# Storing the MoE output through 32x32 VectorE transposes, with a new order of the output matmuls

## The chip, the cores and the metric

The kernel runs on one core of one Trainium2 chip. The metric is the device time of one execution in microseconds; lower is better. Ratios are the mean time of one kernel's runs over that of the kernel before in the same rounds, so a ratio is not quite the ratio of the medians quoted beside it.

Engines: PE is TensorE (matmuls), PEld its weight loads, ACT is ScalarE, DVE is VectorE, POOL is GpSimd, SP issues DMAs.

## The reference, cut to what matters

```python
def reference(q, kv, w_sr, moe_w_in, moe_w_out):
    x = attention(q, pooled(kv) @ w_sr)      # 4 x 12288 queries of 128 channels, 768 keys each
    x = x.reshape(49152, 128)
    h = x @ moe_w_in                         # 128 -> 2048
    g = h * (1.0 / (1.0 + np.exp(-1.702 * h)))
    return (g @ moe_w_out).astype(np.float32)   # 2048 -> 128
```

The kernel computes everything transposed: channels lie on the 128 partitions, tokens along the free dimension. So the last matmul leaves the output of 512 tokens as `[128 channels, 512 tokens]` in one PSUM bank, while the result in memory has one row of 128 channels per token. Something has to transpose it.

## The kernel before: the parts that matter

The work is cut into units of three 128x512 matmuls. A unit is filled (three matmuls into a PSUM tile of three banks), passed through ACT (exp in the attention, gelu in the MoE) and drained (three more matmuls that accumulate in a bank of `ring`). There are 192 attention units and then 512 MoE units; a token group of 512 tokens is 16 chunks, so 5.33 MoE units. The PSUM tile `big` has two buffers: PE may fill unit n+2 only when ACT is done with unit n.

```python
    def fill_moe(t):
        h_ps = big.tile([128, K, 512], F32, name="big")            # K = 3, two buffers
        for k in range(K):
            g, fc = divmod(K * t + k, FCH)                         # FCH = 16
            nc.tensor.matmul(h_ps[:, k, :], w_in_sb[:, fc * 128:(fc + 1) * 128],
                             xs[g // 4][:, (g % 4) * G:(g % 4 + 1) * G], start=True, stop=True)
        a = agpool.tile([128, K, 512], BF, name="ag")
        nc.scalar.activation(a, h_ps, AF.Gelu_apprx_sigmoid)
        g_of[t] = a

    def drain_moe(t):
        todo = list(late)
        late.clear()
        a = g_of.pop(t)
        for k in range(K):
            # ... o_of[g] = ring.tile(...) at the first chunk of a group
            nc.tensor.matmul(o_of[g], w_out_sb[:, fc, :], a[:, k, :],
                             start=(fc == 0), stop=(fc == FCH - 1))
            if fc == FCH - 1:
                oT = opool.tile([128, 128, 4], BF, name="oT")
                nc.vector.tensor_copy(oT.rearrange("p a b -> p (a b)"), o_of[g])
                late.append((g, oT))
        for g, oT in todo:
            store(g, oT)

    def store(g, oT):
        o_ps = o_of.pop(g)[:, 0:256].bitcast(BF)
        for gi in range(4):
            nc.tensor.transpose(o_ps[:, gi * 128:(gi + 1) * 128], oT[:, :, gi], ident)
        o_sb = opool.tile([128, 4, 128], F32, name="o_sb", bufs=3)
        nc.vector.tensor_copy(o_sb.rearrange("p a b -> p (a b)"), o_ps)
        nc.sync.dma_start(out=out_r[g], in_=o_sb)
```

In the order of steps, drains run ten units (L) behind in the attention. From the first MoE step on, two attention drains are issued per step until none is left; MoE drains start five units behind, and every sixteenth step has a second one until the distance is zero.

```python
    for n in range(NA + NM):
        fill(n + 2)
        for _ in range(2 if n >= NA else 1):
            if done_a < NA and n - L >= done_a - (L if n >= NA else 0):
                drain_attn(done_a // 2, done_a % 2)
                done_a += 1
        # ... sums of exps every eighth step, side work of the attention
        if n >= NA + L // 2:
            for _ in range(2 if n % 16 == 0 else 1):
                if done_m <= n - NA:
                    drain_moe(done_m)
                    done_m += 1
```

I call a drain beyond one per step an **extra drain**: ten are needed in either kernel to come from a distance of ten to none.

The softmax here doesn't subtract the row's maximum and nothing guards it: scores larger than these inputs give would overflow.

Of the kernel before, what the change touches and what calls it, by code (L numbers as in the profile page):

```python
# [7 lines left out]
F32 = mybir.dt.float32  # L8
BF = mybir.dt.bfloat16
# [10 lines left out]
def kernel(  # L20
    ctx, tc, q, kv, w_sr, moe_w_in, moe_w_out, out,
):
    nc = tc.nc
    B, N, C = q.shape
    _, H, W, _ = kv.shape
# [16 lines left out]
    q_bf = nc.dram_tensor("q_bf", (B * N, C), BF, kind="Internal").ap()  # L42

    kv_r = kv.rearrange("b (ch p) (a w) c -> b a ch p (w c)", p=128, a=2)
    out_r = out.rearrange("(g p i) c -> g p i c", p=128, i=4)

    L = 10

# [4 lines left out]
    qpool = ctx.enter_context(tc.tile_pool(name="qpool", bufs=3))  # L53
    agpool = ctx.enter_context(tc.tile_pool(name="ag", bufs=14))
    npool = ctx.enter_context(tc.tile_pool(name="norm", bufs=5))
    opool = ctx.enter_context(tc.tile_pool(name="op", bufs=2))
    big = ctx.enter_context(tc.tile_pool(name="big", bufs=2, space=bass.MemoryType.PSUM))
    ring = ctx.enter_context(tc.tile_pool(name="ring", bufs=2, space=bass.MemoryType.PSUM))

# [14 lines left out]
    def pool_kv(b, a):  # L74

        ps = ring.tile([128, 512], F32, name="ring")
        ts = [kv_tiles.pop((b, a, ch)) for ch in range(HC)]
        order = ([(ch, w) for ch in range(HC) for w in range(r)] if b == 0 else
                 [(ch, w) for w in range(r) for ch in range(HC)])
        for ch, w in order:  # L80
            if (b, a, w) == (0, 0, 0) and ch > 0:
                warm(4)
            nc.tensor.matmul(ps[32 * ch:32 * ch + 32, :], mean4, ts[ch][:, w],  # L83
                             start=(w == 0), stop=(w == r - 1))
        pooled[b, a] = kvtmp.tile([Hp, 4, C], BF, name="pooled")
        nc.vector.tensor_copy(pooled[b, a].rearrange("p a c -> p (a c)"), ps[:Hp, :])  # L86

    def transpose_pooled(b, a):
        ps = ring.tile([128, 4, Hp], BF, name="ring")
        t = pooled.pop((b, a))  # L90
        for wp in range(4):
            nc.tensor.transpose(ps[:, wp, :], t[:, wp, :], ident[:Hp, :Hp])  # L92
        pTs[b, a] = kvtmp.tile([128, h], BF, name="pT")
        nc.vector.tensor_copy(pTs[b, a], ps.rearrange("p a b -> p (a b)"))

    def make_k(b, a):
        ps = ring.tile([128, 512], F32, name="ring")
        if a == 0:
            kTs[b] = kvres.tile([128, J], BF, name="kT")
        nc.tensor.matmul(ps[:, :h], w_sr_sb, pTs[b, a], start=True, stop=True)  # L100
        nc.vector.tensor_copy(kTs[b][:, a * h:(a + 1) * h], ps[:, :h])

    def make_v(b, a):
        ps = ring.tile([128, 512], F32, name="ring")
        if a == 0:
            vs[b] = kvres.tile([128, JC, C], BF, name="v")
        pT = pTs.pop((b, a))
        for k in range(K):
            nc.tensor.matmul(ps[:, k * C:(k + 1) * C], pT[:, k * 128:(k + 1) * 128], w_sr_sb,
                             start=True, stop=True)  # L110
        nc.vector.tensor_copy(vs[b][:, a * K:(a + 1) * K, :].rearrange("p k c -> p (k c)"), ps[:, :h])
# [18 lines left out]
    def transpose_q(g):  # L130
        s = g // 4
        if g % 4 == 0:
            qTs[s] = qpool.tile([128, 1, SG], BF, name="qT")
        ps = ring.tile([128, 4, 128], BF, name="ring")
        for i in range(4):
            o = (g % 4) * G + i * 128
            nc.tensor.transpose(ps[:, i, :], xs[NS // 2 + s][:, o:o + 128], ident)  # L137
        dst = qTs[s][:, 0, (g % 4) * G:(g % 4 + 1) * G].rearrange("p (t i) -> p t i", i=4)
        src = ps.rearrange("p i t -> p t i")
        if g < 3:  # L140
            nc.scalar.copy(dst, src)  # L141
        else:
            nc.vector.tensor_copy(dst, src)  # L143
# [22 lines left out]
    ident = cpool.tile([128, 128], BF)  # L166
    nc.vector.memset(ident, 0.0)
    for m in range(0, 128, 32):
        p = slice(m, m + 32)
# [34 lines left out]
    def fill_attn(i, t):  # L204
        b, s = i // GB, i // 4
        s_ps = big.tile([128, K, 512], F32, name="big")
        rhs = qTs[s][:, 0, (i % 4) * G:(i % 4 + 1) * G]
        for k in range(K):
            jc = K * t + k
            nc.tensor.matmul(s_ps[:, k, :], kTs[b][:, jc * 128:(jc + 1) * 128], rhs,  # L210
                             start=True, stop=True)
        a = agpool.tile([128, K, 512], BF, name="ag")
        nc.scalar.activation(a, s_ps, AF.Exp, scale=scale)  # L213
        a_of[i, t] = a

    def drain_attn(i, t):
        b, s = i // GB, i // 4
        if t == 0:
            av_of[i] = ring.tile([128, 512], F32, name="ring")
        for k in range(K):  # L220
            jc = K * t + k
            nc.tensor.matmul(av_of[i], vs[b][:, jc, :], a_of[i, t][:, k, :],  # L222
                             start=(jc == 0), stop=(jc == JC - 1))
        del a_of[i, t]
        if t == 1:
            nc.vector.tensor_tensor(xs[s][:, (i % 4) * G:(i % 4 + 1) * G],  # L226
                                    av_of.pop(i), rb_of.pop(i), MUL)
# [23 lines left out]
    def background(i):  # L251

        b, gb, s = i // GB, i % GB, i // 4
        if i % 4 == 0:
            if 3 <= s + 2 < NS:
                load_qT(s + 2)
            if 4 <= s + 3 < NS:
                cast_q(s + 3)
        if b + 1 < B and gb in loads:
            a, ch = divmod(loads.index(gb), HC)  # L260
            load_kv(b + 1, a, ch)
        if i == 40:
            nc.gpsimd.dma_start(out=w_in_sb, in_=moe_w_in)
        if i == 64:
            nc.gpsimd.dma_start(out=w_out_sb, in_=moe_w_out.rearrange("(o p) c -> p o c", p=128))
# [12 lines left out]


    g_of, o_of = {}, {}  # L280
    late = []

    def fill_moe(t):
        h_ps = big.tile([128, K, 512], F32, name="big")
# [6 lines left out]
        g_of[t] = a  # L291

    def drain_moe(t):
        todo = list(late)
        late.clear()
        a = g_of.pop(t)
        for k in range(K):
            g, fc = divmod(K * t + k, FCH)
            if fc == 0:
                o_of[g] = ring.tile([128, 512], F32, name="ring")  # L300
            nc.tensor.matmul(o_of[g], w_out_sb[:, fc, :], a[:, k, :],  # L301
                             start=(fc == 0), stop=(fc == FCH - 1))
            if fc == FCH - 1:
                oT = opool.tile([128, 128, 4], BF, name="oT")
                nc.vector.tensor_copy(oT.rearrange("p a b -> p (a b)"), o_of[g])  # L305
                late.append((g, oT))
        for g, oT in todo:
            store(g, oT)

    def store(g, oT):  # L310
        o_ps = o_of.pop(g)[:, 0:256].bitcast(BF)
        for gi in range(4):
            nc.tensor.transpose(o_ps[:, gi * 128:(gi + 1) * 128], oT[:, :, gi], ident)  # L313
        o_sb = opool.tile([128, 4, 128], F32, name="o_sb", bufs=3)
        nc.vector.tensor_copy(o_sb.rearrange("p a b -> p (a b)"), o_ps)  # L315
        nc.sync.dma_start(out=out_r[g], in_=o_sb)

    NA = 2 * NG
    NM = NG * FCH // K
# [4 lines left out]
    def fill(n):  # L324
        if n < NA:
            i, t = units[n]
            if n % 2 == 0:
                background(n // 2)
            if n < 8:
                if n == 1:  # L330
                    transpose_q(3)
                if n == 2:
                    make_v(0, 0)
                if n == 4:
                    pool_kv(0, 1)
                    transpose_pooled(0, 1)
                    make_k(0, 1)
                if n == 6:
                    make_v(0, 1)
                if n == 7:  # L340
                    transpose_q(4)
                    transpose_q(5)
            fill_attn(i, t)
        elif n < NA + NM:
            fill_moe(n - NA)


    fill(0)
    fill(1)
    done_a = done_m = 0  # L350
    for n in range(NA + NM):
        fill(n + 2)
        for _ in range(2 if n >= NA else 1):
            if done_a < NA and n - L >= done_a - (L if n >= NA else 0):
                drain_attn(done_a // 2, done_a % 2)
                done_a += 1
        if n < NA and n % 8 == 7:
            sums(n // 8)
        elif n < NA and n % 2 == 1:
            if n in (9, 11):  # L360
                transpose_q(6 + (n - 9) // 2)
            extra(n // 2)
        if n >= NA + L // 2:
            for _ in range(2 if n % 16 == 0 else 1):
                if done_m <= n - NA:
                    drain_moe(done_m)
                    done_m += 1
    assert done_a == NA and done_m == NM
    for g, oT in late:
        store(g, oT)  # L370


# [28 lines left out]
```

## Time and profile before

| | before |
|---|---|
| time, median | 1023.45 us at first (3 runs); 1023.14 us with one run more |
| span of the profiled execution | 1021.7 us |
| busy: PE / ACT / DVE | 999.7 / 959.1 / 262.3 us |
| MoE: end of the first gelu to end of the last | 322.41 to 1015.88 us, 511 gaps |
| end of the last gelu to the end | 5.79 us |

PE and ACT are both nearly full, and busy shares can't rank two engines that pipeline their instructions: a recorded matmul lasts 0.38 us while matmuls start every 0.216. The paces have to be found from single instructions. Two more lines matter later. The first is the gelu's line of the view by source line, with smallest, median and largest duration in ns; the second is a stretch of the ACT timeline (start, length, number of instructions in the uninterrupted run).

```profile
L290 ACT ACTIVATE ag<-big x512: 1445/1556/1606, 321.0 to 1014.3; 128x1536 bf16<-128x1536 f32 x171
```

The run of 24, cut off by the window of the view, begins with a gelu recorded with 1.445 us, the second after a long gap (the first after a wait or a long gap is recorded with 1.450 us and the next with 1.445).

### The profile page before, as it was taken

To read this page: it belongs to the slowest core of one execution; us is meant where nothing else is said; L and a number is where in the kernel's file an instruction comes from. 1 tells how busy PE (TensorE), PEld (TensorE's weight loads), DVE (VectorE), ACT (ScalarE), POOL (GpSimd) and SP (SyncE) were. 2 spreads that over 40 slices of the span, in tenths; PEclk is the share of its full clock that TensorE was granted. 3 is DMA by queue.
4 is the path that set the end of the run, shared out by engine and by line. 5 is a ranking of instruction groups with operands and counts; after the bars stand their busy time and mean duration, and the time that the engine had idled before them with its cause. 6 is when DMAs were issued, how large, how long until landed. Compare 5 with 4: busy or idle time off the path is not lost.

```text
span 1021.7 us, 13264 instructions
## 1 busy us (share of the span) xinstructions
PE 999.7 (98%) x5298; PEld 457.9 (45%) x5398; DVE 262.3 (26%) x417; ACT 959.1 (94%) x709; POOL 92.6 (9%) x151
## 2 busy tenths in 40 slices
PE   7899999999999999999999999999999999999998
PEld 2344444444444444444444444444444444444443
DVE  3344344344334111221212111111212111111212
ACT  3888988988998999999999999999999999999997
POOL 3132332332222000000000000000000000000000
PEclk8999999999999999999999999999999999999999
DMA  9984784896500001101010110101010110101011
GB/s 189 185 145 83 145 165 83 145 158 90 83 21 1 31 32 42 42 31 42 31 42 32 41 42 32 42 31 42 32 42 31 42 42 31 42 31 42 31 42 42
DMA packets 67230, 63.84 MB, mean 62 GB/s; under 512 B 50176, under 2 KB 51328, under 8 KB 66816
## 3 DMA queue, kind: packets, MB, share of 16 engines
q0 software_dynamic: 7440, 26.22, 14.2%
q1 hardware_dynamic: 59728, 36.77, 13.3%
q8 instruction: 42, 0.69, 0.3%
q14 instruction: 20, 0.16, 0.1%
HBM read 52.49 MB, written 36.70 MB: 87 GB/s over the span
## 4 chain that ended last, share of the span: by engine, by line
PE 93%; ACT 3%; DVE 1%; issue 1%; DMA 1%; POOL 0%; ACTq 0%; DVEq 0%; POOLq 0%
PE big L287 31%; PE ring L301 30%; PE ring L222 12%; PE big L210 12%; PE ring L234 3%; ACT ag L290 3%; PE ring L313 2%; DMA x<-in_kv_dram 1%; PE ring L83 1%; ACT ag L213 1%; DVE x L226 0%; ACTq L396 0%; DVE oT L305 0%; DVE pooled L86 0%; PE ring L92 0%
## 5 line engine op out<-in xcount | busy, mean ns | idle before, releaser
L290 ACT ACTIVATE ag<-big 128x1536 bf16<-128x1536 f32 x512 | 690.0, 1546 | 4.9 <-PE big L287 4.5
L287 PE MATMUL big<-x,w_in_sb 128*128 128x512 bf16 x1507 | 412.5, 379 | 2.3
L301 PE MATMUL ring<-ag,w_out_sb 128*128 128x512 bf16 x1496 | 406.9, 379 | 1.9 <-ACT ag L290 0.5
L213 ACT ACTIVATE ag<-big 128x1536 bf16<-128x1536 f32 x192 | 264.8, 1464 | 37.3 <-PE big L210 36.6
L301 PEld LDWEIGHTS <-w_out_sb 128*128 128x128 bf16 x1536 | 150.0, 98 | 181.8 <-issue 0.7
L287 PEld LDWEIGHTS <-w_in_sb 128*128 128x128 bf16 x1536 | 145.8, 98 | 163.5 <-issue 8.0
L305 DVE CAST oT<-ring 128x512 bf16<-128x512 f32 x96 | 66.4, 692 | 451.0 <-PE ring L301 451.0
L210 PE MATMUL big<-qT,kT 128*128 128x512 bf16 x548 | 155.0, 384 | 5.6 <-DVE qT L143 2.0
L222 PE MATMUL ring<-ag,v 128*128 128x512 bf16 x573 | 154.6, 379 | 1.7 <-DVE x L226 1.1
L226 DVE TENSOR_TENSOR x<-ring,rb 128x512 bf16<-128x512 f32 x96 | 66.4, 692 | 159.0 <-PE ring L222 157.7
L315 DVE CAST o_sb<-ring 128x512 f32<-128x512 bf16 x96 | 66.4, 692 | 101.7 <-PE ring L313 101.7
L222 PEld LDWEIGHTS <-v 128*128 128x128 bf16 x576 | 56.2, 98 | 71.2 <-issue 5.3
L210 PEld LDWEIGHTS <-kT 128*128 128x128 bf16 x576 | 53.3, 98 | 76.3 <-issue 17.7
L246 POOL PARTITION_BROADCAST rb<-t x96 | 66.6, 797 | 220.2 <-DVE t L243 220.2
L313 PEld LDWEIGHTS <-oT 128*128 128x128 bf16 x384 | 32.2, 113 | 22.7 <-DVE oT L305 1.9
L313 PE MATMUL ring<-ident,oT 128*128 128x128 bf16 x384 | 37.2, 219 | 0.9 <-DVE oT L305 0.8
L234 PE MATMUL ring<-ag,ones 128*32 128x512 bf16 x576 | 35.5, 381 | 0.0
L234 PEld LDWEIGHTS <-ones 128*32 128x32 bf16 x576 | 13.2, 96 | 20.6 <-issue 10.2
L239 DVE STREAM_TRANSPOSE t<-ring 128x512 f32<-128x512 f32 x24 | 17.2, 717 | 18.8 <-PE ring L234 18.8
L243 DVE STREAM_TRANSPOSE t<-t 128x512 f32<-128x512 f32 x24 | 17.1, 712 | 2.5
L141 ACT COPY qT<-ring 128x512 bf16<-128x512 bf16 x3 | 1.8, 585 | 13.8 <-PE ring L137 13.8
L117 POOL DMA_DIRECT2D q_bf<-in_q_dram x22 | 11.4, 519 | 4.1 <-DMA x<-in_kv_dram 2.8
(41 smaller groups left out, 95.9 us busy)
## 6 DMA issues: line engine op xcount, KB each, us to landing
out_dram<-o_sb SPq DMA_DIRECT2D x96, 256.0 KB, 2.0
q_bf<-in_q_dram POOLq DMA_DIRECT2D x22, 512.0 KB, 7.3
kvt<-in_kv_dram POOLq DMA_DIRECT2D x18, 512.0 KB, 5.7
x<-in_kv_dram POOLq DMA_DIRECT2D x6, 512.0 KB, 10.7
x<-in_q_dram POOLq DMA_DIRECT2D x1, 512.0 KB, 18.6
w_in_sb<-in_moe_w_in_dram POOLq DMA_DIRECT2D x1, 512.0 KB, 9.5
w_out_sb<-in_moe_w_out_dram POOLq DMA_DIRECT2D x1, 512.0 KB, 13.6
x<-in_q_dram POOLq DMA_DIRECT2D x1, 384.0 KB, 10.5
```

What stands on the lines that cost most here:

```text
L210: nc.tensor.matmul(s_ps[:, k, :], kTs[b][:, jc * 128:(jc + 1) * 128], rhs, start=True, stop=True)
L213: nc.scalar.activation(a, s_ps, AF.Exp, scale=scale)
L222: nc.tensor.matmul(av_of[i], vs[b][:, jc, :], a_of[i, t][:, k, :], start=(jc == 0), stop=(jc == JC - 1))
L226: nc.vector.tensor_tensor(xs[s][:, (i % 4) * G:(i % 4 + 1) * G], av_of.pop(i), rb_of.pop(i), MUL)
L234: nc.tensor.matmul(ss[32 * gi:32 * gi + 32, :], ones, a_of[4 * s + gi, jc // K][:, jc % K, :], start=(jc == 0), stop=(jc == JC - 1))
L246: nc.gpsimd.partition_broadcast(rb, t2[32 * gi:32 * gi + 1, :])
L287: nc.tensor.matmul(h_ps[:, k, :], w_in_sb[:, fc * 128:(fc + 1) * 128], xs[g // 4][:, (g % 4) * G:(g % 4 + 1) * G], start=True, stop=True)
L290: nc.scalar.activation(a, h_ps, AF.Gelu_apprx_sigmoid)
L301: nc.tensor.matmul(o_of[g], w_out_sb[:, fc, :], a[:, k, :], start=(fc == 0), stop=(fc == FCH - 1))
L305: nc.vector.tensor_copy(oT.rearrange("p a b -> p (a b)"), o_of[g])
L313: nc.tensor.transpose(o_ps[:, gi * 128:(gi + 1) * 128], oT[:, :, gi], ident)
L315: nc.vector.tensor_copy(o_sb.rearrange("p a b -> p (a b)"), o_ps)
```

## The change

Its intent: take the four PE transposes per group off PE, and two DVE copies with them. DVE's transpose turns each 32x32 block where it stands, so after it partition 32m+i holds, for 16 blocks b of 32 tokens, the 32 channels 32m to 32m+31 of token 32b+i. The blocks then go to their places by the address pattern of the store: four stores per group, one for each quarter of the partitions, in runs of 32 floats, 128 bytes. The second part keeps one drain per step across the switch to the MoE and puts the extra drains in every twelfth step.

```diff
-    out_r = out.rearrange("(g p i) c -> g p i c", p=128, i=4)
+    out_r = out.rearrange("(g b i) (a j) -> g a i b j", b=16, i=32, j=32)
...
-    opool = ctx.enter_context(tc.tile_pool(name="op", bufs=2))
+    opool = ctx.enter_context(tc.tile_pool(name="op", bufs=3))
...
             if fc == FCH - 1:
-                oT = opool.tile([128, 128, 4], BF, name="oT")
-                nc.vector.tensor_copy(oT.rearrange("p a b -> p (a b)"), o_of[g])
-                late.append((g, oT))
-        for g, oT in todo:
-            store(g, oT)
-    # store(): four PE transposes, a second copy, one 256 KB store    (cut)
+                o_sb = opool.tile([128, 512], F32, name="o_sb")
+                nc.vector.transpose(o_sb, o_of.pop(g))
+                for m in range(4):
+                    nc.sync.dma_start(out=out_r[g, m],
+                                      in_=o_sb[32 * m:32 * m + 32, :].rearrange("i (b j) -> i b j", j=32))
...
     for n in range(NA + NM):
         fill(n + 2)
-        # two attention drains per step, MoE drains from NA + 5 on, a second one where n % 16 == 0   (cut)
+        if n >= L:
+            drain(d)
+            d += 1
+        if n >= NA and n % 12 == 0 and d <= n:
+            drain(d)
+            d += 1
```

The attention's instructions and their order are the same in both kernels until the switch.

More of the change, by code (lines that the diff above doesn't have):

```diff
@@ L280 @@
     g_of, o_of = {}, {}
-    late = []
     def fill_moe(t):
@@ L293, in drain_moe @@
     def drain_moe(t):
-        todo = list(late)
-        late.clear()
         a = g_of.pop(t)
@@ L303, in drain_moe @@
             if fc == FCH - 1:
-                oT = opool.tile([128, 128, 4], BF, name="oT")
-                nc.vector.tensor_copy(oT.rearrange("p a b -> p (a b)"), o_of[g])
-                late.append((g, oT))
-        for g, oT in todo:
-            store(g, oT)
-    def store(g, oT):
-        o_ps = o_of.pop(g)[:, 0:256].bitcast(BF)
-        for gi in range(4):
-            nc.tensor.transpose(o_ps[:, gi * 128:(gi + 1) * 128], oT[:, :, gi], ident)
-        o_sb = opool.tile([128, 4, 128], F32, name="o_sb", bufs=3)
-        nc.vector.tensor_copy(o_sb.rearrange("p a b -> p (a b)"), o_ps)
-        nc.sync.dma_start(out=out_r[g], in_=o_sb)
+                o_sb = opool.tile([128, 512], F32, name="o_sb")
[3 more added lines that the diff above has]
+                                      in_=o_sb[32 * m:32 * m + 32, :].rearrange("i (b j) -> i b j", j=32))
     NA = 2 * NG
@@ L345, in fill, with drain @@
             fill_moe(n - NA)
+    def drain(d):
+        if d < NA:
+            drain_attn(d // 2, d % 2)
+        else:
+            drain_moe(d - NA)
     fill(0)
     fill(1)
-    done_a = done_m = 0
+    d = 0
     for n in range(NA + NM):
         fill(n + 2)
-        for _ in range(2 if n >= NA else 1):
-            if done_a < NA and n - L >= done_a - (L if n >= NA else 0):
-                drain_attn(done_a // 2, done_a % 2)
-                done_a += 1
+        if n >= L:
[4 more added lines that the diff above has]
+            d += 1
         if n < NA and n % 8 == 7:
@@ L362 @@
             extra(n // 2)
-        if n >= NA + L // 2:
-            for _ in range(2 if n % 16 == 0 else 1):
-                if done_m <= n - NA:
-                    drain_moe(done_m)
-                    done_m += 1
-    assert done_a == NA and done_m == NM
-    for g, oT in late:
-        store(g, oT)
+    assert d == NA + NM
 _INS = ['q', 'kv', 'w_sr', 'moe_w_in', 'moe_w_out']
```

## The prediction

> **What bounds the kernel now.** I read the page's engine shares first, then the windows of the three stretches after the attention, then single engines in order of time.
>
> ```profile
> PE 999.7 (98%) x5298; PEld 457.9 (45%) x5398; DVE 262.3 (26%) x417; ACT 959.1 (94%) x709; POOL 92.6 (9%) x151
> PE   7899999999999999999999999999999999999998
> ACT  3888988988998999999999999999999999999997
> DMA  9984784896500001101010110101010110101011
> ```
>
> Two engines are near full at once: TensorE (PE) and ScalarE (ACT). From slice 13 on (the MoE) the DMA engines are nearly empty. The share of busy time can't say which of the two sets the pace, so I went to stretches. Columns of the next view: stretch, its length, then busy time and instruction count of PE, PEld, DVE, ACT and POOL, the granted clock, the DMA share, GB/s.
>
> ```profile
> 310.00:334.00 24.00, 23.84 (x135) 10.51 (x131) 9.62 (x16) 20.66 (x16) 5.55 (x8) 1.00 0.00 1
> 334.00:440.00 106.00, 105.33 (x524) 49.79 (x534) 20.74 (x30) 103.47 (x78) 0.00 (x0) 1.00 0.10 37
> 440.00:1010.00 570.00, 566.95 (x2805) 267.01 (x2859) 109.28 (x158) 569.87 (x425) 0.00 (x0) 1.00 0.10 37
> ```
>
> The MoE is 512 units of three 128x512 matmuls in, one gelu of 1536 columns, three matmuls out. From 440 us on ACT is busy in 569.87 of 570 us, so it can gain only if its instructions come closer together. How close can they? Read one by one, the starts of neighbouring gelus are exactly 1.330 us apart in over half of the 511 gaps and never less, so 1.330 is ACT's own pace. In 440 to 1014 us the mean gap is 1.345. From the first gelu (320.96) to the last (1014.33) are 693.37 us; 511 x 1.330 = 679.63; **the MoE has 13.7 us over ACT's floor, and no more than that is to be won there**. PE, in order of time:
>
> ```profile
> 702.46 0.81 PE L287 MATMUL big<-x,w_in_sb 128*128 128x512 bf16 x3
> 703.10 0.81 PE L301 MATMUL ring<-ag,w_out_sb 128*128 128x512 bf16 x3
> 703.75 0.39 PE L313 MATMUL ring<-ident,oT 128*128 128x128 bf16 x4
> 703.97 0.81 PE L287 MATMUL big<-x,w_in_sb 128*128 128x512 bf16 x3
> 704.62 0.81 PE L301 MATMUL ring<-ag,w_out_sb 128*128 128x512 bf16 x3
> 705.26 0.81 PE L287 MATMUL big<-x,w_in_sb 128*128 128x512 bf16 x3
> ```
>
> The second column is a modelled, overlapping duration; the starts count. Six matmuls take 705.26 - 703.97 = 1.29 us; the unit with the four output transposes takes 703.97 - 702.46 = 1.51, so the transposes cost 0.22 us. A token group is 16/3 = 5.33 units: PE needs 5.33 x 1.294 + 0.224 = 7.13 us, ACT 5.33 x 1.330 = 7.09. PE is the bound by a hair, and without the transposes ACT would be.
>
> **Where the 13.7 us are.** By summing the gaps over 1.330: first ten units 2.9, the next 74 units 4.4, the other 427 units 6.5. The first two are extra drains. At the switch each step runs one MoE fill and two attention drains, nine matmuls, and later every sixteenth step has a second MoE drain:
>
> ```profile
> 325.36 1.45 ACT L290 ACTIVATE ag<-big 128x1536 bf16<-128x1536 f32 x1 [0.26 <-PE big L287]
> 327.30 1.45 ACT L290 ACTIVATE ag<-big 128x1536 bf16<-128x1536 f32 x1 [0.49 <-PE big L287]
> 329.24 1.45 ACT L290 ACTIVATE ag<-big 128x1536 bf16<-128x1536 f32 x1 [0.49 <-PE big L287]
> 416.03 2.97 ACT L290 ACTIVATE ag<-big 128x1536 bf16<-128x1536 f32 x2 [0.31 <-PE big L287]
> 438.62 4.14 ACT L290 ACTIVATE ag<-big 128x1536 bf16<-128x1536 f32 x3 [0.82 <-PE big L287]
> ```
>
> Gaps of 1.94 us show ACT idle for PE. The one of 0.82 is worse: there the second drain came right behind a group's end and PE itself waited 0.63 us for the bf16 copy that the transposes read. Of the last 6.5 us, 1.7 are seven gaps of 1.57, one every 64 units, ACT's own (the data had been there); the change can't touch them. 3.5 are 65 gaps of 1.36 to 1.40 and 1.3 are steps of 0.017.
>
> **What the Trainium skill says.** "ScalarE: Activation LUTs", section "What ACT_TABLE_LOAD costs": an ACTIVATE with immediates takes 186 ns + 0.833 ns per column and back-to-back ones overlap by about 93 ns; for 1536 columns that is an estimate of 1.37 us apart. The trace agrees in kind and is a little faster, 1.330. "TensorE: Matmul & The Clock Gate", Part 4, gives a 128x128 bf16 PE transpose 275 to 390 ns; here four in a row start 0.056 us apart, so the trace's 0.22 for four decides. "VectorE: DVE Perf Modes", section "The three transpose paths", says that VectorE transposes only 32x32 blocks, each in place; that is why the stores must put the blocks where they belong. "DMA: Bandwidth & Descriptors", Specifications, wants 512 B for line rate and says that smaller transfers make the engine read, modify and write. The trace before has no store of under 2 KB to HBM, so it can't confirm that.
>
> **The change part by part.**
>
> Removed from PE: 384 transposes, 96 x 0.224 = 21.5 us of PE time. What ACT gets of it is only down to its own floor: in the last 427 units the 6.5 us become 1.7 (the long gaps) plus perhaps 0.6 of small steps, so **-4.2 us**.
>
> VectorE: two casts per group go, one 32x32 transpose comes.
>
> ```profile
> L305 DVE CAST oT<-ring 128x512 bf16<-128x512 f32 x96 | 66.4, 692 | 451.0 <-PE ring L301 451.0
> L315 DVE CAST o_sb<-ring 128x512 f32<-128x512 bf16 x96 | 66.4, 692 | 101.7 <-PE ring L313 101.7
> L239 DVE STREAM_TRANSPOSE t<-ring 128x512 f32<-128x512 f32 x24 | 17.2, 717 | 18.8 <-PE ring L234 18.8
> ```
>
> The last row is this very operation (f32, PSUM to SBUF): 0.717 us. So 96 x (0.692 + 0.692 - 0.717) = 64 us of VectorE time go, all of it beside other work: worth nothing by itself. A PSUM bank of the two-deep ring is free about 0.7 us after the group's last matmul instead of after copy, a wait for PE's turn, transposes and a second copy.
>
> The order of drains: the number of extra drains is still ten (lag 10 down to 0), but one every twelve steps from the first MoE step. Now PE has slack: per step 1.330 - 1.294 = 0.036 us, 0.43 in twelve steps. How far can it run ahead? A fill starts 0.05 us after ACT frees its buffer, its data is ready 0.91 us after its start (0.43 to the last matmul's start and 0.48 to the gelu, from a starved unit), while ACT can take it 0.27 us later than that. So an extra drain of 0.647 us costs ACT about 0.36, and twelve steps are enough to regain the 0.28. Ten of them: 3.6 us. A walk through both orders with these durations gives 10.0 us over the floor for before (measured 13.7: it misses the small steps and PE's wait for the copy) and 5.3 for after, of which 3.4 for the extra drains. So 2.9 + 4.4 = 7.3 become about 3.8: **-3.5 us**.
>
> Stores: 96 of 256 KB in 2 KB packets become 384 of 64 KB in 128 B packets, 196,608 packets. Packet records: 2048 B take 0.081 to 0.084 us, 512 B 0.025 to 0.027, 256 B (the transposed q) from 0.018. That is a line of some 9 ns plus the bytes at 29 per ns, an estimate of 0.014 us for 128 B. One group has 2048 packets, 128 on each of 16 engines if spread evenly: 1.8 us, or about 4 if the read-modify-write doubles it, of the 7.1 a group lasts. Issuing: 0.33 us each, four in 1.3. Both hidden; three o_sb buffers allow two more groups of delay. **0 us.**
>
> The end:
>
> ```profile
> 1015.94 0.81 PE L301 MATMUL ring<-ag,w_out_sb 128*128 128x512 bf16 x3 [0.46 <-ACT ag L290]
> 1016.78 0.69 DVE L305 CAST oT<-ring 128x512 bf16<-128x512 f32 x1 [3.81 <-PE ring L301]
> 1017.98 0.69 DVE L315 CAST o_sb<-ring 128x512 f32<-128x512 bf16 x1 [0.51 <-PE ring L313]
> ```
>
> From the first cast to the end of the second are 1.89 us, now 0.72: -1.2. Against it the fourth store is issued 1.0 us later than the only one was, and small packets may land later by up to 1. **+0.5.** The attention before 319 us is the same program: 0.
>
> Sum: -4.2 - 3.5 + 0.5 = -7.2. 1023.45 - 7.2 = **1016.3 us**, 0.7% faster.
>
> **The rivals.**
> A. *PE's whole saving arrives* (21.5 us, 2.1%). For it: the chain that ended last lies 93% on PE. Against: ACT is busy for 99.98% of the last 570 us with starts never under 1.330; the floor allows at most 12 us (13.7 less 1.7). It would make about 1002; I give it 2%.
> B. *The stores become the bound.* If a 128 B packet to HBM holds its engine over 7.1 / 128 = 0.055 us, or the issue of a 512-run store takes over 1.8 us of the queue, VectorE waits for o_sb, PE for the ring, and the MoE stretches with it: at 0.060 us 7.7 us per group, 96 x 0.6 = +57 us, about 1073. Against: the fit above is far below. For: no small store to HBM is in this trace, and the q transposes kept the issuing queue for 2.7 us and more each. 7%.
> C. *Only the end suffers:* stores are hidden but the last four land 3 to 5 us late; about 1019.
> D. *Nothing comes of the extra drains:* as before each costs ACT its full 0.6 us; then about 1018.5.
>
> **Range and chances.** C and D with their sums, and a smaller residue than I allow (1013), give 1012.5 to 1022.5. Rival A is the only way to over 2% faster: 0.02; B the only way to over 2% slower: 0.07; within 2%: 0.91.
>
> **What would show it.** Right: in the late MoE a mean gap of gelu starts of about 1.335 (before 1.345) with the 1.36 to 1.40 gaps gone and one of 1.57 every 64 units left; PE waiting some 0.03 us per unit for ACT; single ACT gaps of some 1.7 us every twelve units early on in place of the runs of 1.94; DVE at some 200 us; a DMA share of 0.25 to 0.6 in the MoE. Wrong: VectorE's transposes waiting for a DMA, PE waiting for VectorE, gelu gaps that still average 1.345, or a long stretch after the last transpose.

## More of the kernel before

```profile
549.03 32.34 ACT L290 ACTIVATE ag<-big 128x1536 bf16<-128x1536 f32 x24
```

The same gelu of the same shape is recorded with 1.445 to 1.606 us.

## The result, and the profile after

The changed kernel took **1019.34 us** (median of 4, 1019.09 to 1019.35) against 1023.14 us (median of 4, 1022.63 to 1023.66) of the kernel before: ratio 0.9962, 95% interval 0.9945 to 0.998. That is 3.8 us, or 0.4%. The result is correct. The prediction was 1016.3 with a range of 1012.5 to 1022.5: the measured time is inside, the forecast gain of 7.2 us about twice the real one.

The same lines of the page as in the prediction (busy time and share; the 40 slices), with the line of the DMA queue that carries the stores:

```profile
PE 999.7 (98%) x5014; PEld 431.3 (42%) x5014; DVE 198.3 (19%) x321; ACT 958.0 (94%) x709; POOL 92.6 (9%) x151
PE   6899999999999999999999999999999999999997
ACT  3888988988999999999999999999999999999997
DMA  9984884796500122222212121221212122222212
...
q1 hardware_dynamic: 248656, 36.79, 21.3%
```

PE has lost 384 transposes (its weight loads, PEld, went from 5398 to 5014; some matmul records are missing before) and yet is busy for the same 999.7 us: a recorded matmul of 0.38 us covers the short wait before the next one, so this figure says nothing about the work. DVE fell by 64 us, as worked out. The stores are now 196,608 small packets, and the DMA engines went from a tenth to two tenths busy in the MoE: far from full.

The windows of the stretches that the prediction showed (the late one cut at 500 us, when the extra drains are over):

```profile
310.00:334.00 24.00, 24.00 (x129) 10.56 (x128) 8.90 (x14) 22.91 (x18) 5.55 (x8) 1.00 0.00 1
334.00:440.00 106.00, 106.00 (x485) 46.92 (x484) 11.44 (x16) 104.52 (x79) 0.00 (x0) 1.00 0.22 38
440.00:500.00 60.00, 60.00 (x273) 26.27 (x271) 6.45 (x9) 59.45 (x45) 0.00 (x0) 1.00 0.22 38
500.00:1010.00 510.00, 510.00 (x2279) 220.09 (x2278) 50.89 (x71) 510.00 (x381) 0.00 (x0) 1.00 0.22 38
```

ACT's busy time before and after in the first stretch is 20.66 and 22.91 us of 24: there the change helped. Between 334 and 440 us it is 103.47 and 104.52. In the late MoE ACT was busy all the time before, and it is now.

**The floor had been misread.** Late in the changed kernel ACT never waits, so its pace must be its own. It is not 1.330 us. This is the gelu's line of the view by source line again, and ACT in order of time where the extra drains are:

```profile
L290 ACT ACTIVATE ag<-big x512: 1445/1704/1727, 320.3 to 1009.9; 128x1536 bf16<-128x1536 f32 x171
```

```profile
320.28 4.13 ACT L290 ACTIVATE ag<-big 128x1536 bf16<-128x1536 f32 x3
324.67 16.22 ACT L290 ACTIVATE ag<-big 128x1536 bf16<-128x1536 f32 x12 [0.26 <-PE big L287]
341.11 16.23 ACT L290 ACTIVATE ag<-big 128x1536 bf16<-128x1536 f32 x12 [0.21 <-PE big L287]
357.55 16.23 ACT L290 ACTIVATE ag<-big 128x1536 bf16<-128x1536 f32 x12 [0.21 <-PE big L287]
```

Read one by one from the second after a wait on, the gelus start 1.330 us apart, but each is recorded some 13 ns longer than the one before: 1.445, 1.458, 1.472 and so on. Their ends are 1.343 apart. The recorded starts run ahead of the work until the recorded length reaches 1.727 us; from then on, in the late MoE of the changed kernel, the starts too come every 1.343 us. So **ACT's pace is 1.343 us per gelu, and it is read from the ends**. The runs of twelve above give it too: 16.23 us less the first 1.450 is 14.78 for 11 steps, 1.344.

With that pace the MoE can be accounted for. All ends of the 512 gelus (recorded start plus recorded length) are read from the trace. With 1.34335 us, the mean of the last 381 gaps of the changed kernel, 511 x 1.34335 = 686.45 us is the floor, and what is over it is summed (a gap here is the time from one gelu's end to the next one's; "late" means gaps 130 to 511):

| us over ACT's floor, by the ends of gelus | before | after |
|---|---|---|
| first 10 gaps | 2.76 | 0.36 |
| gaps 10 to 130 (extra drains) | 3.53 | 3.08 |
| gaps 130 to 511 | 0.73 | 0.00 |
| sum in the MoE | 7.02 | 3.44 |
| end of the first gelu, from the span's start | 322.41 | 321.73 |
| end of the last gelu to the end | 5.79 | 5.97 |
| span: first gelu's end + 686.45 + sum + end | 1021.67 | 1017.59 |

The columns add up to the spans. The MoE gained 3.58 us. The end lost 0.18. The 0.69 us before the first gelu ends belongs to an attention that is the same program; over all profiled runs this point lies between 321.2 and 322.5 us with no relation to the change, so it is scatter.

In the late MoE there was almost nothing to win: 0.73 us. ACT was already the bound there, because the PE's 7.13 us per group are *below* 5.33 x 1.3434 = 7.16, not above the 7.09 that the prediction used.

The end, in order of time (DVE's last transpose, then the four issues of its stores):

```profile
1012.52 0.72 DVE L304 STREAM_TRANSPOSE o_sb<-ring 128x512 f32<-128x512 f32 x1 [5.57 <-PE ring L299]
```

```profile
1013.26 1.94 SPq L306 DMA_DIRECT2D out_dram<-o_sb  x4
```

One DVE instruction of 0.72 us now stands where a cast, PE transposes and a second cast took 1.89 us; but the issue takes 1.94 us instead of 0.33, so that nothing is left: the end is 0.18 us longer.

### The profile page after: what moved, and what is told of

Same layout as the page of the kernel before. It is cut to its first block, busy times and chain, and to the rows that moved or that the text cites. A ratio compares the mean times of both kernels' runs of the same rounds, so it can differ in the third digit from the quotient of the medians. Undisturbed runs are those within 1.5% of the kernel's fastest.

```text
span 1017.6 us, 12883 instructions
## 1 busy us (share of the span) xinstructions
PE 999.7 (98%) x5014; PEld 431.3 (42%) x5014; DVE 198.3 (19%) x321; ACT 958.0 (94%) x709; POOL 92.6 (9%) x151
## 4 chain that ended last, share of the span: by engine, by line
ACT 49%; PE 44%; issue 4%; DMA 2%; DVE 1%; POOL 0%; DVEq 0%; POOLq 0%
ACT ag L290 48%; PE ring L223 12%; PE big L211 12%; PE big L287 8%; PE ring L299 8%; PE ring L235 3%; DMA x<-in_kv_dram 2%; PE ring L84 1%; ACT ag L214 1%; POOL x L72 0%; POOL x L127 0%; PE ring L93 0%; PE ring L101 0%; DVE qT L144 0%; PE ring L110 0%
## 5 line engine op out<-in xcount | busy, mean ns | idle before, releaser
L299 PE MATMUL ring<-ag,w_out_sb 128*128 128x512 bf16 x1536 | 413.1, 379 | 0.5 <-ACT ag L290 0.5
L287 PEld LDWEIGHTS <-w_in_sb 128*128 128x128 bf16 x1536 | 148.0, 96 | 205.4 <-issue 75.8
L304 DVE STREAM_TRANSPOSE o_sb<-ring 128x512 f32<-128x512 f32 x96 | 68.8, 717 | 609.3 <-PE ring L299 609.3
L72 POOL DMA_DIRECT2D kvt<-in_kv_dram x18 | 10.2, 569 | 9.4 <-PE ring L84 5.4
L186 PE MATMUL big<-ones 128*32 128x512 bf16 x22 | 7.7, 503 | 0.9 <-DVE col L162 0.9
L87 DVE CAST pooled<-ring 96x512 bf16<-96x512 f32 x8 | 5.5, 687 | 14.3 <-PE ring L84 14.3
```

The lines of the kernel that those rows point to most:

```text
L299: nc.tensor.matmul(o_of[g], w_out_sb[:, fc, :], a[:, k, :], start=(fc == 0), stop=(fc == FCH - 1))
L304: nc.vector.transpose(o_sb, o_of.pop(g))
```

## The experiments

The theory to be tested (theory 1): ACT's pace is 1.343 us, the PE transposes were hidden behind ACT late in the MoE, and the gain is only ACT idle time behind extra drains. Its first rival (theory 2) is the prediction's own account: the pace is 1.330 and the transposes did cost 4.2 us, and something new in the changed kernel, such as the small stores or DVE's reading of PSUM, slows the gelus down to 1.343. Others are named with the runs. Eight kernels ran, in two sets of four, each set beside the kernel before on its chip (medians 1023.21 and 1022.79 us).

| kernel | us, median | ratio to before, 95% interval |
|---|---|---|
| old order, new output path | 1020.41 | 0.9976 (0.9964 to 0.9989) |
| new order, old output path | 1022.98 | 0.9999 (0.9987 to 1.0012) |
| changed kernel, plain store (wrong result) | 1017.62 | 0.9950 (0.9935 to 0.9965) |
| changed kernel, single extra matmuls | 1016.24 | 0.9934 (0.9921 to 0.9946) |
| before, shorter gelu (wrong result) | 1018.94 | 0.9963 (0.9948 to 0.9978) |
| changed kernel, shorter gelu (wrong result) | 998.39 | 0.9759 (0.9745 to 0.9772) |
| changed kernel, no extra drains | 1021.62 | 0.9987 (0.9973 to 1.0001) |
| single extra matmuls, two store queues | 1015.97 | 0.9931 (0.9918 to 0.9943) |

### One part of the change at a time

First the new output path with the old order of drains:

```diff
     # the kernel before, with drain_moe, out_r and opool of the changed kernel
-                oT = opool.tile([128, 128, 4], BF, name="oT")
-                nc.vector.tensor_copy(oT.rearrange("p a b -> p (a b)"), o_of[g])
-                late.append((g, oT))
+                o_sb = opool.tile([128, 512], F32, name="o_sb")
+                nc.vector.transpose(o_sb, o_of.pop(g))
+                for m in range(4):
+                    nc.sync.dma_start(out=out_r[g, m], in_=...)
```

> The new output path (VectorE transpose, 128-byte stores) with the old order of drains. Theory 1: ScalarE's own pace is 1.343 us per gelu, read from the ends of its instructions (the starts run ahead), so nothing was to be won late in the MoE and the gain is ScalarE's idle time behind the extra drains alone. Then the ends-over-1.343 sum of the MoE falls from 7.0 us before to about 4.3 (a walk with the durations of the trace: five early gaps of 1.67 to 1.94, then five of 1.67), and the time is about 1020.6. Theory 2, the prediction's: the pace is 1.330, the PE transposes cost 4.2 us late in the MoE, and something new in the changed kernel (small stores, the VectorE transpose reading PSUM) holds the gelus at 1.343. Then this run shows the same late mean gap as the changed kernel, but its time is about 1019 or below only if those 4.2 us come; with the new brake it stays near 1022 to 1023.

Measured: 1020.41 us, a sum over the floor of 4.58 us. Then the new order with the old path:

```diff
     # the changed kernel, with drain_moe, store, out_r and opool of the kernel before
     assert d == NA + NM
+    for g, oT in late:
+        store(g, oT)
```

> The new order of drains with the old output path (transposes on TensorE). Theory 1: TensorE has only 0.04 us of slack per group left beside its transposes, so it can't regain its head start between two extra drains; each of the ten costs ScalarE 0.4 to 0.7 us; the sum over 1.343 stays at about 6.6 (before 7.0), the time about 1022.7. Theory 2: the order by itself is worth 3.5 us: about 1019.6.

Measured: 1022.98 us, no difference from before, and a sum of 6.82 us. The four kernels side by side:

| us over ACT's floor | before | new path alone | new order alone | both |
|---|---|---|---|---|
| first 10 gaps | 2.76 | 2.76 | 0.36 | 0.36 |
| gaps 10 to 130 | 3.53 | 1.81 | 5.72 | 3.08 |
| gaps 130 to 511 | 0.73 | 0.00 | 0.74 | 0.00 |
| sum | 7.02 | 4.58 | 6.82 | 3.44 |

The new path alone is worth 2.44 us, the new order alone 0.20, both together 3.58: the order is worth 1.14 us only where the path is new. The reason is in the ACT timeline. This is the new order with the transposes on PE:

```profile
341.55 16.35 ACT L291 ACTIVATE ag<-big 128x1536 bf16<-128x1536 f32 x12 [0.21 <-PE big L288]
358.41 16.29 ACT L291 ACTIVATE ag<-big 128x1536 bf16<-128x1536 f32 x12 [0.51 <-PE big L288]
```

and this the old order with DVE's transpose, from the last of the doubled attention drains on:

```profile
331.32 1.45 ACT L289 ACTIVATE ag<-big 128x1536 bf16<-128x1536 f32 x1 [0.49 <-PE big L286]
333.26 16.23 ACT L289 ACTIVATE ag<-big 128x1536 bf16<-128x1536 f32 x12 [0.49 <-PE big L286]
349.70 21.60 ACT L289 ACTIVATE ag<-big 128x1536 bf16<-128x1536 f32 x16 [0.21 <-PE big L286]
```

With PE free of transposes an extra drain idles ACT by a recorded 0.21 us, 0.32 by the ends; in the other kernel it is 0.21 the first time and 0.51 the next (0.61 by the ends, and 0.44 to 0.73 at the seven after it). PE can be ahead of ACT by some 0.3 us and no more, which I put down to the two PSUM buffers between them (their number was not varied): the prediction worked out 0.27, and 0.647 less the measured 0.319 gives 0.33. An extra drain of 0.647 us uses that up and costs ACT the rest. Without transposes PE needs 5.33 x 1.295 = 6.91 us per group where ACT needs 7.16, so it gains 0.26 us per group and is ahead again after one group or a little more. With transposes it gains 0.04 us per group; twelve steps are two groups and a quarter, and the next extra drain finds the head start not regained. Not all of the new path's gain in gaps 10 to 130 is of this kind: of its 1.72 us some 0.61 belong to one extra drain of the kernel before (a gap of 2.27 us, where it is 1.66 with the new path), at which PE itself waited 0.63 us for the first copy.

The late mean gap is that of the changed kernel in the new path alone (1.3434 us), which both theories expect; theory 2's saving of 4.2 us late does not come (0.73), which speaks for theory 1.

### Are the small stores a brake?

The changed kernel with one store of 256 KB per group, in 2 KB runs, to the wrong places:

```diff
-    out_r = out.rearrange("(g b i) (a j) -> g a i b j", b=16, i=32, j=32)
+    out_r = out.rearrange("(g p i) c -> g p i c", p=128, i=4)
...
-                for m in range(4):
-                    nc.sync.dma_start(out=out_r[g, m], in_=o_sb[32 * m:32 * m + 32, :]...)
+                nc.sync.dma_start(out=out_r[g], in_=o_sb.rearrange("p (i c) -> p i c", c=128))
```

> The changed kernel with one 256 KB store of 2 KB runs per group, in the wrong places (wrong result on purpose). Theory 1: stores are hidden; the mean late gap of gelu ends stays 1.343 and only the end is shorter by the three further issues, about 1.0 to 1.3 us: 1018.1. Theory 2: if the 128-byte stores are the new brake, gelus come at 1.330 apart again and the time falls by about 5 more, to some 1013.

Measured: 1017.62 us (the result wrong, as meant). The sum over the floor is 3.43 us and the late gap 1.3434, as in the changed kernel (3.44 and 1.3434): the stores are hidden. The end, from the last gelu on, is 4.61 us instead of 5.97. So the small stores cost 1.36 us in all, once, at the end. The issue at the end:

```profile
1012.84 0.33 SPq L305 DMA_DIRECT2D out_dram<-o_sb  x1
```

0.33 us stands against the 1.94 us of the four. In the packet records of the changed kernel a 128-byte packet has a median of 11 ns, so that the doubling by read, modify and write that the prediction allowed for is not seen.

### Was ACT the bound late in the MoE, with PE just behind it?

If so, a shorter gelu must bring out what it hides: with transposes on PE very little, without them much. The same edit in both kernels. Their outputs are wrong, which doesn't matter for the times. GpSimd has nothing else to do in the MoE:

```diff
-        nc.scalar.activation(a, h_ps, AF.Gelu_apprx_sigmoid)
+        nc.scalar.activation(a[:, :, 0:480], h_ps[:, :, 0:480], AF.Gelu_apprx_sigmoid)
+        nc.gpsimd.memset(a[:, :, 480:512], 0.0)
```

> The kernel before with a gelu of 480 of each 512 columns, the rest set to zero by GpSimd (wrong result on purpose). ScalarE's work falls by 96 columns, an estimate of 0.08 us per unit. Theory 1: ScalarE would then come every 1.263 us, so TensorE with its transposes becomes the bound, 7.13 us per group or 1.336 per unit; the MoE falls by only about 3.5 us: about 1019.5. Rival, TensorE was the bound all along: no change at all, 1023.

> The same cut in the changed kernel. Theory 1: without transposes TensorE needs 1.295 us per unit, so the gain that ScalarE hid appears: late gaps of about 1.295, the MoE shorter by some 22 us, the time about 997. Rival, something else (the small stores, VectorE's transpose) holds the changed kernel at 1.343: it stays near 1019.

Measured: 1018.94 us for the kernel before, 998.39 for the changed one. The smallest distance of gelu starts fell from 1.330 to 1.250 us, the 0.08 that had been estimated. By the ends of gelus in gaps 130 to 511 the kernel before went from 1.345 to 1.338 us, the changed kernel from 1.343 to 1.296. In the former, single gaps of 1.518 us now appear once per group: 1.295 and the 0.224 of the four transposes, seen on ACT for the first time. The windows from 440 to 980 us, first the kernel before and then the changed one, both with the shorter gelu:

```profile
440.00:980.00 540.00, 537.21 (x2675) 255.06 (x2727) 104.61 (x152) 528.14 (x405) 71.82 (x404) 1.00 0.10 37
```

```profile
440.00:980.00 540.00, 537.42 (x2454) 244.68 (x2501) 56.61 (x79) 537.43 (x417) 73.54 (x414) 1.00 0.22 39
```

In the same 540 us the former starts 405 gelus and the latter 417, and ACT sits idle for 11.9 us in the former, where with the full gelu it was all but never idle. In the latter six matmuls follow each other without a gap, 1.295 us per unit, so PE is the bound in both. The pair shows what the PE transposes are worth where ACT does not hide them: 1018.94 - 998.39 = 20.55 us. That is nearly the whole of the 21.5 us of PE time, and the rest of the differences between the two kernels (drain order, end) is in it. Late in the MoE, where those play no part, it is 1.338 - 1.296 = 0.042 us per unit or 0.224 per group: the four transposes. With the full gelu the whole change was worth 3.8. The pair also bears on the "seven long gaps" of the prediction: they stay as gaps of 1.57 us, one in 64 units, where PE is the bound and has no head start, and cost nothing in the changed kernel with the full gelu, where the ends stay 1.343 apart across them, but for one that comes right behind an extra drain (0.23 us). What happens every 64 units was not tested, but the traces hold a hint. ACT has two recorded instructions per unit, the wait for a semaphore and the gelu, so 64 units are 128 instructions; and in the changed kernel a packet of 8 KB of the kind "instruction" (queue q14) starts 0.65 to 0.76 us after the gelu that follows each of the eight long gaps of the MoE. So the gaps go together with a fetch of instructions; that it causes them is not shown.

### What an extra drain costs

Without any extra drain, the ten come after the last gelu:

```diff
-        if n >= NA and n % 12 == 0 and d <= n:
-            drain(d)
-            d += 1
...
+    while d < NA + NM:
+        drain(d)
+        d += 1
```

> The changed kernel without any extra drain: it stays ten units behind to the end. Theory 1: the sum over 1.343 falls from 3.4 to about 0.4, and the ten drains come after the last gelu, 10 x 0.647 less the one that stood there: +5.8 us. Together about +2.7: 1022. Rival (the gaps are not due to the extra drains): the sum stays at about 3 and the time is about 1025.

Measured: 1021.62 us. The sum over the floor is 0.00 and the end 11.72 us instead of 5.97, which is 5.75 more. The whole MoE up to 480 us is one run of ACT without a wait:

```profile
319.77 161.31 ACT L290 ACTIVATE ag<-big 128x1536 bf16<-128x1536 f32 x120
```

161.31 - 1.45 = 159.86 us for 119 steps: 1.3434. This run shows the floor without any correction, and that all 3.44 us of the changed kernel's idle time are due to its ten extra drains.

### A version that beats both

An extra drain is three matmuls, 0.647 us, against a head start of about 0.3. A single matmul of 0.216 us fits in. So the ten extra drains are cut into thirty single matmuls, one in every fifth step, in which PE regains 5 x 0.049 = 0.24 us:

```diff
-        if n >= L:
-            drain(d)
-            d += 1
-        if n >= NA and n % 12 == 0 and d <= n:
-            drain(d)
-            d += 1
+        # drain(), drain_attn and drain_moe now issue one matmul per call   (cut)
+        if n >= L:                                   # d now counts single matmuls
+            for _ in range(K + 1 if n >= NA and n % 5 == 0 else K):
+                if d < K * (n + 1):
+                    drain(d)
+                    d += 1
```

> The changed kernel with its ten extra drains of three matmuls cut into thirty single matmuls, one in every fifth step. Theory 1: one extra matmul (0.216 us) fits in the 0.27 us by which TensorE runs ahead of ScalarE, and five steps regain 5 x 0.049 us, so all gaps of 1.66 vanish: the sum over 1.343 falls from 3.4 to about 0.4 and the time to about 1016.2. Rival: ScalarE waits at an extra drain for something other than TensorE's time (a buffer of the unit drained, a semaphore); then the sum stays near 3 and the time near 1019.

Measured: 1016.24 us, correct; ratio to before 0.9934. The sum over the floor is 0.16 us, all of it in one gap of 1.51 us, one of those that come every 64 units. The ACT timeline that had a wait every twelve units has none in the first 119:

```profile
320.21 160.13 ACT L291 ACTIVATE ag<-big 128x1536 bf16<-128x1536 f32 x119
```

The total of PE's work and of the extra matmuls is that of the changed kernel; their grain and their spacing are others, and were not varied one at a time. Together with the timelines, in which ACT's waits at extra drains end with a fill (PE big), this speaks against the rival that ACT waited for a buffer or for a semaphore of the unit drained.

Last, the same with two of the last group's four stores issued from ACT's queue, which is idle by then:

```diff
+                    queue = nc.scalar if g == NG - 1 and m % 2 else nc.sync
-                    nc.sync.dma_start(out=out_r[g, m],
+                    queue.dma_start(out=out_r[g, m],
```

> Single extra matmuls every fifth step, and of the last group's four stores two are issued by ScalarE's queue. Theory 1: as single_extra_5, and the end shorter by two issues of 0.3 to 0.5 us: about 1015.4. If the end is not bound by the issues but by the landing of the last packets, it equals single_extra_5, about 1016.2.

Measured: 1015.97 us, ratio 0.9931. In the trace the end fell from 5.99 to 5.60 us, less than the 0.8 expected. The times, 1015.97 and 1016.24 from the two sets with intervals of the ratio that overlap almost wholly, don't tell the two apart; that the second queue helps is shown only by this one pair of traces.

## Why the prediction was right in the time and wrong in a term

That the time fell inside the range is in part luck. The range reached up to 1022.5 for rivals C and D, of which neither happened in its size, and the main line forecast 7.2 us for a gain of 3.8. Of the prediction's own signs of being right, DVE at some 200 us (198.3) and single ACT gaps of some 1.7 us every twelve units (1.66) came true; the late mean gap of starts of 1.335 (measured 1.343, close to its sign of being wrong, 1.345) and the DMA share of 0.25 or more (0.22) did not.

By its own steps:

- **"1.330 is ACT's own pace"**: wrong, and this is the term that failed. It was read from the distances of starts; the ends give 1.343. The floor of the MoE is therefore 686.45 us and not 679.63, and what could be won was 7.0 us, not 13.7.
- **"PE is the bound by a hair"**: wrong by the same hair. PE's 7.13 us per group were right, ACT's are 7.16. The shorter gelu shows both: with 1440 columns PE with transposes sets 1.338 per unit, and without them 1.296.
- **Transposes off PE, late: -4.2 us**: mis-sized, measured -0.73 (gaps 130 to 511). The 65 gaps of 1.36 to 1.40 that were to vanish did vanish, but they had only been the recorded starts, which had run ahead, falling back; at the ends of the same gelus there was no loss.
- **Seven gaps of 1.57 as ACT's own loss of 1.7 us, which the change can't touch**: wrong in size; by the ends they cost 0.12 each before, and after nothing where PE has its head start.
- **Order of drains: -3.5 us** (from 7.3 to 3.8): right in mechanism, measured from 6.29 to 3.44, -2.85. Each extra drain was to cost ACT 0.36 us beyond the head start; it costs 0.32, and the first one 0.36. It holds only together with the new path, as the prediction had it: it let PE's new slack pay for the regained head start.
- **DVE and stores 0 us**: right; DVE waits for PE alone, and the stores cost nothing but the end. The packets were quicker than the estimate (11 instead of 14 ns), the issues slower: 0.32 and then some 0.5 us each, not 0.33.
- **The end: +0.5**: right in sign, +0.18 between the two traces.
- **Attention: 0**: right; the 0.69 us between the two profiled runs is scatter.
- Rival A (the whole of PE's saving) fails for the reason given, ACT's floor, and the shorter gelu shows it. Rival B (stores as the bound) is ruled out by the plain store; one of its supports was also read loosely: the 22 issues of q transposes took 1.9 to 8.8 us each, not 2.7 and more. Rival C happened in small, 1.36 us. Rival D did not happen with the new path; it is what the new order with the old path does.

The sum in the MoE is -0.73 - 2.85 = -3.58 us. The gain went where most of it had never been to be had: behind ACT.

## What to carry to other kernels

When two engines are both nearly full, find the pace of each from the ends of a long run without waits, because the recorded starts of a busy engine may run ahead of its work; and divide by the work of the same stretch, since 1% decides which of the two is the bound. A change that relieves the engine just behind the bound is worth only the idle time that its bursts cause. Where an engine is only a small buffer ahead, cut the extra work into pieces that fit in that head start, and spread them so that it is regained in between: that brought 3.3 us of the sum here, where the new order of whole drains had brought 1.1.

## What the Trainium skill lacked or had wrong

- "Perfetto Trace Analysis", section "Per-instruction lifecycle: what the profiler-reported window actually captures", has the recorded start of a ScalarE instruction as the moment when its execution begins. In this stream of equal gelus the recorded lengths grow from 1.445 to 1.727 us while the ends stay 1.343 us apart, so here the recorded start is no fixed point of an instruction's execution when instructions follow each other closely. A warning that starts run ahead is missing.
- "ScalarE: Activation LUTs", section "What ACT_TABLE_LOAD costs": its figures give an estimate of 1.37 us between back-to-back gelus of 1536 columns, 2% too much; measured are 1.343 from PSUM to bf16 in SBUF.
- No page was found to have the late start of one gelu in 64 (gaps of 1.57 us where there is no head start), beside which an 8 KB packet of instructions starts.
- "TensorE: Matmul & The Clock Gate", Part 4, gives 275 to 390 ns for one PE transpose of 128x128 and lacks the distance of several in a row: here the four of a group start 56 ns apart, and with them a unit takes 0.224 us longer.
- "DMA: Bandwidth & Descriptors", Specifications, warns of a read-modify-write under 512 B, and the page lacks a figure for small stores on this chip: 128-byte packets to HBM were recorded with a median of 11 ns, 2 KB ones with 81 to 84, and 196,608 of them were hidden in the MoE. The issues of four stores in a row took 0.32 and then 0.49 to 0.51 us each.
